# One PSUM bank for a step's transposes of p, copied by one engine in turn, and other places for two weight loads

## The chip, the cores and the metric

The kernel runs on one core of a Trainium2 chip. The metric is the device time of one execution in microseconds. Three runs of the kernel before gave 422.18, 422.83 and 426.23, a median of 422.83.

## The reference: what is computed

Three layers follow each other, all in fp32.

```
attention: B,H,S,D = 4,8,576,64; causal window of 128, bias -slope_h*(i-j)
    attn = softmax(q k^T / sqrt(D) + bias);  x = attn v          # 2304 tokens x 512
soft MoE: logits = x phi (512 x 32); dispatch = softmax over tokens, combine = softmax over slots
    slot_input = dispatch^T x;  slot_out[e] = relu(slot_input[e] w1[e]) w2[e]   # 8 experts, 512 -> 1024 -> 512
    x = combine slot_out
last layer: h = relu(x w_in) (512 x 2048);  out = (h*h) w_out
```

## The kernel before, in words

Four stages follow each other: attention, the sums that lead from the tokens to the 32 slots, the 16 + 16 weight tiles of the experts (w1, w2, 1 MB each), and the last layer, a long run of matmuls (L735).

**Attention** works on 16 pairs u (a batch and two heads). A pair has nine chunks of 64 queries. The two heads lie over each other in the 128 partitions, and a chunk looks at no more than 192 keys. Two chunks make a step, so there are 72 steps t. One step goes through all engines: TensorE makes the scores s (`emit_S`, L162); VectorE adds the bias and takes the maximum (`emit_max`, L170); ScalarE takes the exponential with its sum (`emit_exp`, L181); VectorE adds 1e-9 and inverts the sum (`emit_add` L185, `emit_norm` L189); GpSimd multiplies p by it (L194); TensorE transposes p in 128 x 128 pieces (`emit_T`, L213 to L221); and the transposes are copied from PSUM into the buffer ptb (`emit_evac`, L235 and L237). When a pair has all its steps in ptb, TensorE multiplies them with V (`emit_PV`, L247). Three steps later the result is turned back into rows (`emit_xn`: four transposes into X, L279, and one into Y, L281; VectorE copies X at L283, ScalarE copies Y at L284). After each fourth pair the logits and the dispatch sums of a batch follow (L267 to L330).

The order of every engine's work is the order in which the loop from L394 writes it down. In one turn t stand: scores of t+1, the transposes of step t-3 (LT is 3), PV where a pair is done, ScalarE's copy, the maximum of t, the sum of t-1, the exponential of t, the inverse and the multiplication of t-1, VectorE's copy, and then the side work such as `emit_xn`. Each engine takes its instructions strictly in this order.

PSUM has eight banks of 512 columns. Three of them carry the tag T, and they are handed out in turn to everything of that tag: each asks for the bank that was handed out three requests earlier, and its first matmul waits until that one has been copied out. Before, a step asks twice: `tp` gets the whole 128 x 128 pieces (one or two), `tq` the half pieces (one or two, of which 64 partitions are used). ScalarE copies `tp` with one instruction, VectorE copies `tq` with one for each half. X, Y and the second result bank of PV (`xb`) have tag T as well.

**Loads** stand in SyncE's queue. When the scores of the last chunk of pair u are made, the loop (L398 to L402) asks for q and k of pair u+2, and then for one weight tile, or two with pairs 2 and 6. V of a later pair follows after `emit_xT`. The tiles go into a ring of 19 buffers, of which the loop fills 18; the rest is asked for by `pump` when the matmuls of the experts have used a tile up. Five more w1 tiles (L82) go where the attention's buffers were.

Of the kernel before, what the change touches and what calls it, by code (L numbers as in the profile page):

```python
# [24 lines left out]
LT = 3  # L25
# [3 lines left out]
def attn_moe_relu2_kernel(ctx: ExitStack, tc: tile.TileContext, z0, q, k, v, phi, w1, w2, w_in, w_out, bias, cst, out):  # L29
# [8 lines left out]

    NBUF = {"S": 3, "T": 3, "xa": 1, "B": 1}

    def bank(tag, name):
        return psum[0].tile([128, 512], F32, tag=tag, name=name, bufs=NBUF[tag])
# [22 lines left out]
    def load_next_w():  # L65
        key = wq.pop(0)
        used[0] += 1
        if key[0] in ("w1", "w2"):
            t = ring.tile([128, 4, 512], F32, tag="w", name=f"w_{key[0]}{key[1]}")
            sp.dma_start(out=t, in_=wsrc[key[0]][key[1]].rearrange("p (a b) -> p a b", a=4))  # L70
        else:
            t = ring.tile([128, 2, 512, 2], I32, tag="w", name=f"f{key[1]}")
            for a, src in enumerate((w_in, w_out)):
                sp.dma_start(out=t[:, a].rearrange("p a b -> p (a b)"), in_=src[key[1]].bitcast(I32))
        wt[key] = t

    def load_extra(n):
        p = more.enter_context(tc.tile_pool(name=f"more{len(extra)}", bufs=n))
        for _ in range(n):
            key = extra.pop(0)  # L80
            wt[key] = p.tile([128, 4, 512], F32, tag="w", name=f"w_{key[0]}{key[1]}")
            sp.dma_start(out=wt[key], in_=wsrc[key[0]][key[1]].rearrange("p (a b) -> p a b", a=4))  # L82
# [37 lines left out]
    ptb = apool.tile([128, 4 * NBL, 128], F32, name="ptb")  # L120
# [14 lines left out]
    def load_q(u):  # L135
        z = zq[u % NQ]
        sp.dma_start(out=z[0:64, :, 0, :], in_=q[u, 0:64].rearrange("p (c t) -> p c t", t=64))
        sp.dma_start(out=z[64:128, :, 1, :], in_=q[u, 64:128].rearrange("p (c t) -> p c t", t=64))
        load_k(u)
# [7 lines left out]
    NS = NCH * NU // 2  # L147
    info = []
    for g in range(2 * NS):
        u, c = divmod(g, NCH)  # L150
# [4 lines left out]
    st_t, sb_t, xa_t, xb_t, tp_t = {}, {}, {}, {}, {}  # L155

    def emit_S(t):
        sb_t[t] = bank("S", "s")
        st_t[t] = apool.tile([128, 6], F32, tag="st", name="st", bufs=4)
        for i in range(2):  # L160
            u, c, n, e = info[2 * t + i]
            pe.matmul(out=sb_t[t][:, 256 * i:256 * i + n], lhsT=zq[u % NQ][:, c].rearrange("p a b -> p (a b)"),  # L162
                      rhs=kt_t[u][:, 64 * c + 64 - n:64 * c + 64], start=True, stop=True)

    def emit_max(t):
        for i in range(2):
            u, c, n, e = info[2 * t + i]
            p = pbuf[t % NP][:, e:e + n]
            pr = u % NPAIR
            dve.tensor_tensor_reduce(  # L170
                out=p, in0=sb_t[t][:, 256 * i:256 * i + n], in1=tbl[:, 192 * pr + 192 - n:192 * pr + 192],
                scale=-0.125, scalar=3.0e38, op0=ALU.add, op1=ALU.min, accum_out=st_t[t][:, i:i + 1],
            )
        sb_t.pop(t)

    def emit_exp(t):
        st = st_t[t]
        for i in range(2):
            u, c, n, e = info[2 * t + i]
            p = pbuf[t % NP][:, e:e + n]  # L180
            act.activation(out=p, in_=p, func=AF.Exp, bias=st[:, i:i + 1], scale=-1.0, accum_out=st[:, 2 + i:3 + i])  # L181

    def emit_add(t):
        st = st_t[t]
        dve.tensor_scalar(out=st[:, 2:4], in0=st[:, 2:4], scalar1=1e-9, scalar2=None, op0=ALU.add)  # L185

    def emit_norm(t):
        st = st_t.pop(t)
        dve.reciprocal(out=st[:, 4:6], in_=st[:, 2:4])  # L189
        for i in range(2):  # L190
            u, c, n, e = info[2 * t + i]
            p = pbuf[t % NP][:, e:e + n]
            eng = dve if t >= NS - 2 and i == 1 else pool
            eng.tensor_scalar(out=p, in0=p, scalar1=st[:, 4 + i:5 + i], scalar2=0.0, op0=ALU.mult, op1=ALU.add)  # L194
# [3 lines left out]
    def emit_T(t):  # L198
        full, half, P = [], [], pbuf[t % NP]
        for u, c, n, e in info[2 * t:2 * t + 2]:  # L200
            if c % 2:
                full.append((jblk(u, c // 2) + 1, e + n - 128))
                if n == 192:
                    half.append((64, jblk(u, c // 2 - 1) + 3, e))
            else:
                half.append((0, jblk(u, c // 2), e + n - 64))
                if n == 192:
                    full.append((jblk(u, c // 2 - 1) + 2, e))
        full.sort(key=lambda x: x[0])
        A = bank("T", "tp")[:, 0:256].rearrange("p (a b) -> p a b", a=2)  # L210
        B = bank("T", "tq")[:, 0:256].rearrange("p (a b) -> p a b", a=2)
        for i, (slot, e) in enumerate(full):
            pe.transpose(A[:, i, :], P[:, e:e + 128], ident)  # L213
        if len(half) == 2 and half[0][0] != half[1][0]:
            pe.transpose(B[:, 0, :], P[:, 128:256], ident)  # L215
            dst = [(ptb[r:r + 64, slot], B[r:r + 64, 0]) for r, slot, e in half]
        else:
            dst = []
            for i, (r, slot, e) in enumerate(half):
                assert r == 0 and e <= 256  # L220
                pe.transpose(B[:, i, :], P[:, e:e + 128], ident)  # L221
                dst.append((ptb[0:64, slot], B[0:64, i]))
        sl = [x[0] for x in full]
        st = sl[1] - sl[0] if len(sl) == 2 else 1
        if st < 0:
            raise AssertionError
        tp_t[t] = [(ptb[:, sl[0]:sl[-1] + 1:st], A[:, 0:len(sl)])], dst

    def jblk(u, j):
        return 4 * ((5 * u + j) % NBL)  # L230

    def emit_evac(t, i):
        for dst, src in tp_t[t][i]:
            if i == 0:
                act.activation(out=dst, in_=src, func=AF.Copy)  # L235
            else:
                dve.tensor_copy(out=dst, in_=src)  # L237

    def emit_PV(u):
        xa_t[u], xb_t[u] = bank("xa", "xa"), bank("T", "xb")  # L240
        for j in range(5):
            pt = ptb[:, jblk(u, j):jblk(u, j) + 4]
            for a, b in ((0, 4),) if j < 3 else ((0, 2), (2, 3)) if j == 3 else ((0, 1),):
                for h in range(2):
                    po = 64 * h
                    out = xa_t[u][po:po + 64, 128 * j + 64 * a:128 * j + 64 * b] if j < 3 or (j == 3 and a == 0) else xb_t[u][po:po + 64, 0:64]
                    pe.matmul(out=out, lhsT=v_t[u][:, j, po:po + 64], rhs=pt[:, a:b, po:po + 64],  # L247
                              start=(j == 0 or (j == 3 and a == 2)), stop=(j == 4 or (j == 3 and a == 0)), skip_group_check=True)
        xT[u] = xT_buf[u % NPAIR]
# [12 lines left out]
    def emit_logits(u):  # L262
        b, kk = divmod(u, NPAIR)
        if kk == 0:
            L_t[b] = bank("B", "L")
        for g in range(4):
# [91 lines left out]
    for u in range(NU):  # L358
# [19 lines left out]
        if u % NPAIR == NPAIR - 1:  # L378
            b = u // NPAIR
# [7 lines left out]
    def run_side(t):  # L387
        for f, a in side.get(t, ()):
            f(*a)
            if f is emit_xT and a[0] + NQ < NU:  # L390
                load_v(a[0] + NQ)

    emit_S(0)
    for t in range(NS + LT + 1):  # L394
        if t + 1 < NS:
            emit_S(t + 1)
            for u, c, n, e in info[2 * t + 2:2 * t + 4]:
                if c == NCH - 1:  # L398
                    if u + NQ < NU:
                        load_q(u + NQ)  # L400
                    for _ in range(2 if u in (2, 6) else 1):
                        load_next_w()  # L402
        if 0 <= t - LT < NS:
            emit_T(t - LT)
        for a in side0.get(t, ()):
            emit_PV(*a)
        if 0 <= t - LT < NS:
            emit_evac(t - LT, 0)
        if t < NS:
            emit_max(t)  # L410
        if 0 <= t - 1 < NS:
            emit_add(t - 1)
        if t < NS:
            emit_exp(t)
        if 0 <= t - 1 < NS:
            emit_norm(t - 1)
        if 0 <= t - LT < NS:
            emit_evac(t - LT, 1)
        run_side(t)
        if t == NS - 2:  # L420
            zt.close()
            load_extra(1)
        if t == NS + LT - 1:
            pt.close()
            load_extra(1)
# [10 lines left out]
    u, b = NU - 1, NB - 1  # L436
    p = slice(32 * b, 32 * b + 32)
# [13 lines left out]
    sl = slice(128 * kk, 128 * kk + 128)  # L451
# [448 lines left out]
```

## Time and profile before

| | |
|---|---|
| runs | 422.18, 422.83, 426.23 us |
| profiled execution | 423.25 us, its span 421.5 us |
| busy over the span | TensorE 400.4 us (95%), VectorE 293.4 (70%), ScalarE 249.7 (59%), GpSimd 94.6 (22%) |
| L213/L215/L221, transposes of p | 128 of `tp`, mean 277 ns |
| L235, ScalarE's copies of `tp` | 72, 25.3 us |
| L237, VectorE's copies of `tq` | 128, 35.4 us |
| bytes moved | 70.95 MB, mean 168 GB/s |

The profiled execution took 0.42 us more than the median of the runs. Busy time counts a matmul until its result is written, so short waits of TensorE can hide in it: a group of matmuls that could have started earlier shows as idle only what is left after the one ahead has drained.

### The profile page before, as it was taken

Reading aid. Unit: us, or ns where it says so; the run is one execution under the profiler, and the core shown is the slowest. Engines: PE = TensorE matmul, PEld = TensorE weight load, DVE = VectorE, ACT = ScalarE, POOL = GpSimd, SP = SyncE. Lnnn points to the kernel's source line nnn. Section 1 sums busy time; section 2 is a strip of 40 time slices with the busy share of each in tenths; the row PEclk is TensorE's granted clock in tenths of the full one; section 3 lists DMA queues with packets and bytes.
Section 4 is the critical chain, followed back from the end, with each engine's and each line's share of the span. In section 5 each row is a group of like instructions: output and inputs, shape, how many; then the busy total and the mean of one; then the engine's idle time right before and its main releaser. Section 6 shows DMA issues by size and latency. Waiting matters only on the chain.

```text
span 421.5 us, 7942 instructions
## 1 busy us (share of the span) xinstructions
PE 400.4 (95%) x2623; PEld 306.7 (73%) x2623; DVE 293.4 (70%) x966; ACT 249.7 (59%) x761; POOL 94.6 (22%) x193
## 2 busy tenths in 40 slices
PE   5999997999999999978999999999999999999996
PEld 4878866878867633356778788787878888888885
DVE  6887777778788426587868768677676676548445
ACT  3888876778777402057766766666666645435341
POOL 4445334244334010146112210111100000000000
PEclk9999999999999999999999999999999999999999
DMA  7979769869686799999602202000000012004004
GB/s 215 307 276 305 261 218 323 218 194 313 223 287 233 264 425 423 412 409 408 255 0 101 100 2 100 2 0 0 2 1 2 1 64 87 0 2 150 0 2 150
DMA packets 35514, 70.95 MB, mean 168 GB/s; under 512 B 19856, under 2 KB 21008, under 8 KB 31376
## 3 DMA queue, kind: packets, MB, share of 16 engines
q1 hardware_dynamic: 35328, 70.30, 47.7%
q8 instruction: 21, 0.34, 0.4%
q14 instruction: 21, 0.17, 0.1%
q10 hardware_dynamic: 144, 0.13, 0.1%
HBM read 65.70 MB, written 4.72 MB: 167 GB/s over the span
## 4 chain that ended last, share of the span: by engine, by line
PE 51%; DVE 2%; issue 1%; POOL 1%; ACT 1%; DVEq 0%; POOLq 0%
PE acc L735 45%; PE h L692 4%; PE MX L644 1%; DVE psum L753 1%; PE MY L650 1%; POOL arena_y L605 1%; DVE arena_y L621 1%; DVE arena_y L619 0%; ACT whl L637 0%; DVE Mst L653 0%; DVE arena_co L623 0%; ACT psum L745 0%; ACT siT L745 0%; DVE arena_gh L721 0%; DVEq L896 0%
## 5 line engine op out<-in xcount | busy, mean ns | idle before, releaser
L735 PE MATMUL acc<-whl,arena_gh 128*128 128x512 f32 x864 | 214.4, 396 | 2.3 <-DVE arena_gh L721 1.8
L735 PEld LDWEIGHTS acc<-whl,arena_gh 128*128 128x128 f32 x864 | 159.9, 189 | 34.8 <-issue 2.8
L721 DVE TENSOR_TENSOR arena_gh<-hT,arena_gh 128x384 fp32r<-128x384 f32 (+1 forms) x95 | 52.7, 555 | 38.5 <-ACT arena_gh L717 34.1
L194 POOL TENSOR_SCALAR p<-p,st 128x192 f32<-128x192 f32 (+1 forms) x142 | 56.1, 408 | 77.0 <-PE s L162 20.2
L704 ACT ACTIVATE acc<-h 128x384 f32<-128x384 f32 (+2 forms) x49 | 23.8, 485 | 75.0 <-PE h L692 75.0
L181 ACT ACTIVATE p<-p,st 128x192 f32<-128x192 f32 (+1 forms) x144 | 61.3, 428 | 8.0 <-DVE st L170 7.3
L162 PE MATMUL s<-kt,zq 128*128 128x192 f32 (+2 forms) x288 | 58.8, 328 | 7.4 <-DMA kt<-in_k_dram 7.0
L605 POOL TENSOR_SCALAR arena_y<-f 128x512 f32<-128x512 f32 x32 | 27.9, 875 | 120.7 <-DVE arena_cin L623 59.0
L162 PEld LDWEIGHTS s<-kt,zq 128*128 128x128 f32 x288 | 44.8, 195 | 10.1 <-DMA zq<-in_z_dram 4.6
L237 DVE COPY ptb<-tq 64x128 f32<-64x128 f32 x128 | 35.4, 281 | 22.1 <-PE tq L215 18.9
L170 DVE CUSTOM_DVE_ANT_0 p<-s,tbl 128x192 f32<-128x192 f32 (+1 forms) x144 | 41.6, 324 | 2.3 <-PE s L162 1.8
L235 ACT ACTIVATE ptb<-tp 128x256 f32<-128x256 f32 (+1 forms) x72 | 25.3, 351 | 19.4 <-PE tp L213 18.1
L247 PE MATMUL xa<-ptb,vt 128*64 128x256 f32 (+1 forms) x256 | 27.8, 359 | 0.0
L213 PE MATMUL tp<-cs,p 128*128 128x128 f32 x128 | 26.4, 277 | 1.3 <-DVE ptb L237 0.7
L181 ACT ACTIVATION_READ_ACCUMULATOR p<-p,st 128x1 f32 x144 | 27.2, 189 | 0.0
L692 PE MATMUL h<-cst_sb,Mst 128*128 128x384 f32 x96 | 25.2, 341 | 1.9 <-DVE Mst L653 1.8
L713 DVE TENSOR_TENSOR hT<-acc 128x384 f32<-128x384 f32 (+1 forms) x18 | 10.2, 566 | 23.4 <-ACT acc L704 23.4
L717 ACT ACTIVATE arena_gh<-acc 128x384 fp32r<-128x384 f32 (+2 forms) x49 | 24.9, 508 | 0.6
L717 ACT ACTIVATE arena_gh<-hT 128x384 fp32r<-128x384 f32 x48 | 24.9, 518 | 0.6
L621 DVE SCALAR_TENSOR_TENSOR arena_y<-f,arena_y 128x512 int32<-128x512 int32 x32 | 24.1, 753 | 1.1
L247 PEld LDWEIGHTS xa<-ptb,vt 128*64 128x64 f32 x256 | 17.0, 136 | 9.6 <-issue 2.4
L692 PEld LDWEIGHTS h<-cst_sb,Mst 128*128 128x128 f32 x96 | 18.1, 190 | 7.1 <-DVE Mst L653 3.3
(171 smaller groups left out, 475.3 us busy)
## 6 DMA issues: line engine op xcount, KB each, us to landing
w_w<-in_w_dram SPq DMA_DIRECT2D x32, 1024.0 KB, 8.1
f<-in_w_in_dram SPq DMA_DIRECT2D x16, 512.0 KB, 10.2
f<-in_w_out_dram SPq DMA_DIRECT2D x16, 512.0 KB, 10.2
vt<-in_v_dram SPq DMA_DIRECT2D x16, 320.0 KB, 6.2
zq<-in_q_dram SPq DMA_DIRECT2D x30, 144.0 KB, 4.3
kt<-in_k_dram SPq DMA_DIRECT2D x15, 288.0 KB, 4.4
out_dram<-psum SPq DMA_DIRECT2D x11, 256.0 KB, 2.1
out_dram<-xn_all SPq DMA_DIRECT2D x4, 256.0 KB, 2.1
```

The source lines that it names most:

```text
L162: pe.matmul(out=sb_t[t][:, 256 * i:256 * i + n], lhsT=zq[u % NQ][:, c].rearrange("p a b -> p (a b)"), rhs=kt_t[u][:, 64 * c + 64 - n:64 * ...
L170: dve.tensor_tensor_reduce(out=p, in0=sb_t[t][:, 256 * i:256 * i + n], in1=tbl[:, 192 * pr + 192 - n:192 * pr + 192], scale=-0.125, scalar ...
L181: act.activation(out=p, in_=p, func=AF.Exp, bias=st[:, i:i + 1], scale=-1.0, accum_out=st[:, 2 + i:3 + i])
L194: eng.tensor_scalar(out=p, in0=p, scalar1=st[:, 4 + i:5 + i], scalar2=0.0, op0=ALU.mult, op1=ALU.add)
L237: dve.tensor_copy(out=dst, in_=src)
L247: pe.matmul(out=out, lhsT=v_t[u][:, j, po:po + 64], rhs=pt[:, a:b, po:po + 64], start=(j == 0 or (j == 3 and a == 2)), stop=(j == 4 or (j ...
L605: pool.tensor_scalar(out=y[:, a].bitcast(F32), in0=t[:, a, :, 1].bitcast(F32), scalar1=2.0 ** -112, scalar2=0.0, op0=ALU.mult, op1=ALU.add)
L621: dve.scalar_tensor_tensor(out=y[:, h], in0=t[:, h, :, 1], scalar=-0x80000000, in1=y[:, h], op0=ALU.bitwise_and, op1=ALU.bitwise_or)
L692: pe.matmul(out=hb[hf][:, 0:HB], lhsT=Mst[:, 128 * f:128 * f + 128], rhs=cst_sb[:, c0:c0 + HB], start=True, stop=True)
L717: act.activation(out=lo_t[i][1][hf][:, 0, cl], in_=rbuf[hf][:, cl], func=AF.Square)
L721: eng.tensor_tensor(out=gh[hf][:, 1, cl], in0=g[hf][:, cl], in1=gh[hf][:, 0, cl].bitcast(F32), op=ALU.subtract)
L735: pe.matmul(out=acc_t[s], lhsT=gh[:, x, c0:c0 + 128], rhs=w[:, f % 2, y, :], start=(f in firsts and a == 0), stop=(f in lasts and a == 2))
```

## The change

Both kinds of pieces of a step now lie in one bank, whole ones in columns 0 to 255 and half ones in columns 256 to 511, so a step asks once for a bank of tag T. All copies of an even step are made by ScalarE, where its copy stood, and all copies of an odd step by VectorE, where its copies stood. The second weight tile of a turn is asked for with pairs 7, 11 and 13 in place of 2 and 6, so 19 tiles are in the ring when the attention ends.

```diff
-        A = bank("T", "tp")[:, 0:256].rearrange("p (a b) -> p a b", a=2)
-        B = bank("T", "tq")[:, 0:256].rearrange("p (a b) -> p a b", a=2)
+        AB = bank("T", "tp").rearrange("p (x a b) -> p x a b", x=2, a=2)
+        A, B = AB[:, 0], AB[:, 1]
...
-        tp_t[t] = [(ptb[:, sl[0]:sl[-1] + 1:st], A[:, 0:len(sl)])], dst
+        tp_t[t] = [(ptb[:, sl[0]:sl[-1] + 1:st], A[:, 0:len(sl)])] + dst
...
-    def emit_evac(t, i):
-        for dst, src in tp_t[t][i]:
-            if i == 0:
+    def emit_evac(t):
+        for dst, src in tp_t.pop(t):
+            if t % 2 == 0:
                 act.activation(out=dst, in_=src, func=AF.Copy)
             else:
                 dve.tensor_copy(out=dst, in_=src)
...
-                    for _ in range(2 if u in (2, 6) else 1):
+                    for _ in range(2 if u in (7, 11, 13) else 1):
                         load_next_w()
...
-        if 0 <= t - LT < NS:
-            emit_evac(t - LT, 0)
+        if 0 <= t - LT < NS and (t - LT) % 2 == 0:
+            emit_evac(t - LT)
...
-        if 0 <= t - LT < NS:
-            emit_evac(t - LT, 1)
+        if 0 <= t - LT < NS and (t - LT) % 2:
+            emit_evac(t - LT)
```

VectorE in the turns 32 and 33 of the loop, from the sum of step 31 to the copy of X of pair 5 (p_96 is p of step 33; `tq` and `tp` are the transposes of step 29, then of step 30). Before:

```order
L185 TENSOR_SCALAR st<-st 128x2
L189 RECIPROCAL st<-st 128x2
L237 COPY ptb<-tq 64x128 x2
L170 ISA p_96,st<-s,tbl 128x192
L170 ISA st 128x1
L170 ISA p_96,st<-s,tbl 128x192
L170 ISA st 128x1
L185 TENSOR_SCALAR st<-st 128x2
L189 RECIPROCAL st<-st 128x2
L237 COPY ptb<-tq 64x128 x2
L283 COPY xn_all<-X 128x4x128
```

And now:

```order
L185 TENSOR_SCALAR st<-st 128x2
L189 RECIPROCAL st<-st 128x2
L237 COPY ptb<-tp 128x2x128
L237 COPY ptb<-tp 64x128 x2
L170 ISA p_96,st<-s,tbl 128x192
L170 ISA st 128x1
L170 ISA p_96,st<-s,tbl 128x192
L170 ISA st 128x1
L185 TENSOR_SCALAR st<-st 128x2
L189 RECIPROCAL st<-st 128x2
L283 COPY xn_all<-X 128x4x128
```

The odd step 29 now has three copies here where it had two, and the even step 30 has none.

ScalarE in the turns 31 to 33 at the same place, from pair 5's result to the exponentials of step 32 (p_94 is step 31, p_95 step 32; the copies are of steps 28, 29 and 30). Before:

```order
L256 ACTIVATE xT_100<-xb 128x64
L235 ACTIVATE ptb<-tp 128x2x128
L181 ACTIVATE p_94,st<-p_94,st 128x192
L181 ACTIVATE p_94,st<-p_94,st 128x64
L235 ACTIVATE ptb<-tp 128x2x128
L181 ACTIVATE p_95,st<-p_95,st 128x128
L181 ACTIVATE p_95,st<-p_95,st 128x192
L235 ACTIVATE ptb<-tp 128x2x128
```

And now:

```order
L256 ACTIVATE xT_100<-xb 128x64
L235 ACTIVATE ptb<-tp 128x2x128
L235 ACTIVATE ptb<-tp 64x128 x2
L181 ACTIVATE p_94,st<-p_94,st 128x192
L181 ACTIVATE p_94,st<-p_94,st 128x64
L181 ACTIVATE p_95,st<-p_95,st 128x128
L181 ACTIVATE p_95,st<-p_95,st 128x192
L235 ACTIVATE ptb<-tp 128x2x128
L235 ACTIVATE ptb<-tp 64x128 x2
```

Two half copies now stand ahead of the exponentials of the odd step 31, and no copy stands ahead of those of step 32.

## Rows read from the trace of the kernel before

**Rows 1.** Windows by stage: busy us (instructions) of each engine, granted clock, DMA share, GB/s.

```profile
3.00:140.00 137.00, 128.95 (x1137) 103.69 (x1138) 105.48 (x598) 101.53 (x422) 56.17 (x143) 1.00 0.83 259
148.20:178.80 30.60, 30.57 (x273) 10.06 (x274) 13.86 (x46) 3.68 (x9) 3.51 (x4) 1.00 1.01 420
197.00:421.00 224.00, 219.41 (x1065) 177.83 (x1064) 152.77 (x277) 129.14 (x291) 21.73 (x25) 1.00 0.14 54
```

**Rows 2.** Timeline, GpSimd: the first work on the last layer's weights.

```profile
176.59 0.68 POOL L605 TENSOR_SCALAR arena_y<-f 128x512 f32<-128x512 f32 x1 [19.36 <-DMA f<-in_w_in_dram]
```

**Rows 3.** Waits of TensorE, 3 to 140 us: total, times, longest.

```profile
PE s L162 <- DMA kt<-in_k_dram: 7.0, 4, 3.4
PE X L279 <- DVE ptb L237: 1.8, 8, 0.3
PE tp L213 <- DVE ptb L237: 0.7, 3, 0.2
PE tq L215 <- DVE ptb L237: 0.3, 2, 0.2
```

**Rows 4.** Timeline, SyncE's queue and TensorE around pair 6's second weight tile: start, us.

```profile
58.28 1.24 SPq L70 DMA_DIRECT2D w_w<-in_w_dram  x2
...
63.26 0.54 SPq L137 DMA_DIRECT2D zq<-in_q_dram  x1
...
70.99 0.54 SPq L137 DMA_DIRECT2D zq<-in_q_dram  x1
...
73.05 0.41 PE L162 MATMUL s<-kt,zq 128*128 128x64 f32 x2 [2.10 <-DMA kt<-in_k_dram]
...
81.63 0.55 SPq L137 DMA_DIRECT2D zq<-in_q_dram  x1
```

**Rows 5.** Timeline, TensorE: X and Y of pair 5, transposes of steps 31, 32.

```profile
61.84 0.63 PE L279 MATMUL X<-cs,xT 128*128 128x128 f32 x4 [0.19 <-DVE ptb L237]
62.30 0.27 PE L281 MATMUL Y<-cs,xT 128*128 128x128 f32 x1
...
63.28 0.30 PE L213 MATMUL tp<-cs,p 128*128 128x128 f32 x1
...
64.10 0.38 PE L213 MATMUL tp<-cs,p 128*128 128x128 f32 x2
```

**Rows 6.** Timeline, VectorE, same steps.

```profile
59.72 0.59 DVE L237 COPY ptb<-tq 64x128 f32<-64x128 f32 x2 [1.39 <-PE tq L215]
...
61.12 0.57 DVE L237 COPY ptb<-tq 64x128 f32<-64x128 f32 x2
...
62.48 0.17 DVE L189 RECIPROCAL st<-st 128x2 f32<-128x2 f32 x1
62.56 0.57 DVE L237 COPY ptb<-tq 64x128 f32<-64x128 f32 x2
```

**Rows 7.** Timeline, ScalarE and GpSimd, same steps.

```profile
59.61 0.38 ACT L235 ACTIVATE ptb<-tp 128x256 f32<-128x256 f32 x1 [0.47 <-PE tp L213]
59.89 0.45 ACT L181 ACTIVATE p<-p,st 128x192 f32<-128x192 f32 x1
...
60.57 0.19 ACT L181 ACTIVATION_READ_ACCUMULATOR p<-p,st 128x1 f32 x1
...
62.81 0.77 POOL L194 TENSOR_SCALAR p<-p,st 128x128 f32<-128x128 f32 x2 [0.70 <-ACT p L181]
```

**Rows 8.** Groups by shape: count, busy us, mean ns.

```profile
L283 DVE COPY xn_all<-X 128x512 f32<-128x512 f32 x15 | 10.3, 685 | 0.8 <-PE X L279 0.6
L284 ACT ACTIVATE xnr<-Y 128x128 f32<-128x128 f32 x15 | 3.9, 261 | 5.0 <-PE Y L281 5.0
L312 DVE COPY dn<-X 128x128 f32<-128x128 f32 x3 | 0.8, 273 | 0.0
```

**Rows 9.** Timeline, VectorE and TensorE: the same place of pair 2, whose step there is odd.

```profile
37.43 0.59 DVE L237 COPY ptb<-tq 64x128 f32<-64x128 f32 x2
...
38.17 0.30 PE L213 MATMUL tp<-cs,p 128*128 128x128 f32 x1 [0.22 <-DVE ptb L237]
```

## The prediction, made before the changed kernel ran

> **What bounds the kernel now.** I began with the windows by stage. In the attention, 3 to 140 us, TensorE is busy 128.95 of 137 us while no other engine passes 105.48, and its clock is full [rows 1]: TensorE's own instructions set the pace and the others have room, on average. From 148 to 179 us the 32 weight tiles run one behind the other (30.57 busy of 30.60), and from 197 us to the end it is again TensorE without holes [rows 1]. Between those two lies a start-up chain of the last layer whose first input is a transfer, at 176.59 us [rows 2]. So nothing behind the attention gets shorter by this change, and whatever the attention gains or loses goes through to the end. The transfers behind it keep up: the first weights of the last layer arrive 2.2 us before the weight matmuls end (178.80), and the change only brings one tile, about 2.5 us of transfer at the 420 GB/s of that window, forward. I price that tile at nothing at the end; its cover is those 2.2 us, and the change makes them longer.
>
> What TensorE waits for inside the attention is the second thing read [rows 3]. Of K it waits 7.0 us in four places. Most of this is the start and stays; one place is 2.10 us at 73.05 us [rows 4]. For banks it waits 1.8 us at eight X, 0.7 us at three `tp` and 0.3 us at two `tq`. That is only the visible part: before X at 61.84 TensorE was idle for 0.19 us, but the copy that released it ended at 61.12 + 0.57 = 61.69, so a release takes 0.15 us, and the transposes ahead were draining in that time.
>
> Third, the queues at one such place [rows 5 to 7]. X of pair 5 waits for VectorE's copies of step 29. The next `tp` at 63.28 waits for those of step 30, which end at 62.56 + 0.57 = 63.13, plus the same 0.15. So the banks that hurt belong to the step directly ahead, not to an old one.
>
> **Part 1, weight tiles.** Pair 6 asks for two tiles at 58.28; q and K for pair 9 are asked for from 63.26 on and TensorE gets K at 73.05, 2.10 us late and 0.15 of drain with it [rows 4]: 2.25 us that go, because pair 6 now asks for one. Pair 7 asks for two instead. The next q and K (for pair 10) are asked for at 70.99 and needed at 81.63, which contains the 2.1: 8.5 us, where the late case had 73.05 - 2.25 - 63.26 = 7.5 and took 9.8 [rows 4]. With the same transfers K would still be 2.25 - 1.0 = 1.25 us late; but the second tile of pair 2 made no wait of that size at all [rows 3], where 3.4 is the start and 2.1 of the rest is pair 6's, with the same loads around it. Between 0 and 1.25 I take the nearer row, pair 2, and put 0.25 us of new waiting for pairs 7 and 11 together (bounds 0 and 2 x 2.25), nothing for pair 13, behind which no q and K follow. Net -2.0 us.
>
> **Part 2, the copies' prices.** VectorE never copies 256 columns in the trace. Nearest rows: 128 columns 273 ns, 512 columns 685 ns [rows 8]; on the line between them 0.41 us (bounds 0.27 and 0.69). ScalarE never copies a half; its 128-column copy takes 261 ns [rows 8], and as its next instruction starts 0.1 us before the end (59.89 against 59.61 + 0.38 [rows 7]) a half occupies it 0.16 us. So ScalarE has 0.32 us more in an even step and 0.28 less in an odd one, VectorE about 0.4 more in an odd one and 0.57 less in an even one. Per two steps the sums hardly move; the order does.
>
> **Part 3, where X follows an even step (pair 5).** Carried through with these prices. ScalarE starts step 28's copies when the last transpose is done, 59.72 (there VectorE began on it [rows 6]) instead of 59.61, and is through with them 0.28 + 0.32 later: the exponentials of step 31 begin at 60.32, not 59.89, and end at 60.57 + 0.19 + 0.43 = 61.19 [rows 7]. VectorE, rid of step 28's copies, stands early before the sum of step 31 and waits for them. Then sum and inverse (0.28), and step 29's copies run from 61.5 to 61.5 + 0.41 + 0.57 = 62.48, against 61.69 before. X no longer needs this bank; now X takes step 28's, and Y takes step 29's. Y goes at 62.63, not 62.30 [rows 5]. Y and the scores behind it take 0.76 us (before, `tp` could have gone at 63.06 and waited 0.22 for its bank), so the next `tp` comes at 63.39 against 63.28: its own wait is gone, and Y's has eaten it. VectorE's inverse of step 32 stands behind step 29's copies and the maximum of 33, and slips from 62.48 to about 63.26; GpSimd follows 0.33 later and needs 0.77 for both halves [rows 6, 7], so the second piece of step 32, wanted 0.11 behind the first at 64.10 + 0.11, is there at 64.36 plus 0.12 for the release. Together the place costs 0.27 us **more** than before: 0.11 at the bank and 0.16 at p.
>
> **Part 4, where it follows an odd step (pair 2).** VectorE's copies for the step start at 37.43 and release `tp` at 38.17 [rows 9]. Now two turns ahead it has 0.4 more, one turn ahead 0.57 less, and the sum waits for exponentials that ScalarE's whole copy has pushed back: the start stays at about 37.4, and with 1.0 us in place of 0.59 plus 0.15 for the release `tp` comes at 38.5. Cost 0.33 us.
>
> Eight places have a wait at X [rows 3]: pairs 0, 1, 5, 9, 13 (even) and 2, 6, 10 (odd) by the parity of the step (9u+8)//2+4. 5 x 0.27 + 3 x 0.33 = +2.3 us. The other pairs have dispatch sums of a batch before or behind X, long matmuls in which VectorE and ScalarE catch up.
>
> **Part 5, what does vanish.** Where a step's `tq` waited for ScalarE's copy of the step before, or for an old copy of VectorE, the next bank is now free: 0.3 us visible in two places plus up to 0.15 of drain each, and more that hides in drain. I take -1.0 us (bounds -0.3 and -2).
>
> **Sum.** -2.0 + 2.3 - 1.0 = -0.7 on the profiled 423.25 us, and this execution lies 0.42 over the median of 422.83: 422.1 us as a median. The sign rests on parts 3 and 4, in which terms of 0.3 us repeat eight times; an error of 0.25 in each is 2 us.
>
> By the Trainium skill, "Perfetto Trace Analysis", section "Optimization Strategy", the same gap that repeats on the engine that should be saturated can mean that there is not enough PSUM for the next tile. The trace has that gap eight times [rows 3]; by that rule one bank less per step removes it, which is the first rival. What speaks against is the release time: 0.15 us behind the copies of the step just ahead.
>
> **Rivals.** (a) **The bank waits go.** If ScalarE's halves delay nothing because exponentials run in holes, then at all eight places the wait at X (1.8 us + 8 x 0.15 = 3.0) and the one behind it (63.28 against about 62.9 without, some 0.3 x 7 = 2.1) disappear. -5.1 - 2.0 - 1.0 = -8.1: 414.7 as a median; half of it 418.8. For it: averages of 74 to 77% for both engines [rows 1]. Against: the carried queues, in which the place of the wait moves by one request. Chance 0.28.
>
> (b) **Slower: p comes late.** Exponentials pushed back (0.43) and long copies of odd steps (0.41) both stand ahead of the inverse, which GpSimd and the transposes of p await. Before, p of step 32 was ready at 62.81 + 0.77 = 63.58, 0.5 ahead of its transposes at 64.10 [rows 5, 7]. If the two delays add up, 0.84 - 0.5 = 0.34, and the bank's 0.33 comes on top, in all 14 pairs with X: +9.4 - 2.0 - 1.0 = +6.4, 429.2. It decides where the delay is over 0.5 us. Chance 0.13.
>
> (c) **K late twice.** If pairs 7 and 11 each cost what pair 6 did, +4.5 - 2.25 + 1.3 = +3.5: 426.4. For it speaks that q and K stand behind two tiles in one queue; by the Trainium skill, "DMA: Bandwidth & Descriptors", section "Queues, rings and completion order", each engine consumes a row's ring in order, so the K has to wait for both, and the late K here agrees (9.8 us from request to use [rows 4]). Against: 8.5 us of room, not 7.5. Chance 0.07.
>
> That leaves 0.52 for the forecast, within 419.5 to 424.5.
>
> **The numbers.** Predicted 422.0 us. Range 416.5 to 426.5: it cuts off the far part of (a), about 0.1, and most of (b), the same. 1% (4.2 us) is about what a measurement of this kernel can tell from no change. Faster by more, below 418.6: (a) but for its weak end, 0.25. Slower by more, over 427.1: (b), 0.12. Within: 0.63.
>
> **What would show it.** In the changed profile: TensorE's K wait at pair 9 gone and none above 0.5 us at pairs 10 and 14; Y, not X, waiting for VectorE's L237 after even steps, for about 0.3 us, and `tp` behind Y after odd ones; ScalarE busy about 4 us more and VectorE about 4 less in the attention; the weight matmuls beginning 0 to 2 us ahead of 148.2; the stages behind unchanged in length. Wrong: no bank waits left and the attention 5 us shorter, or waits of the transposes for GpSimd's p in most pairs.

## The result and the profile after

The changed kernel takes **425.75 us** (median of 22 runs, 424.88 to 427.7) against 422.76 of the kernel before in the same runs (22 runs, 421.3 to 426.23): a ratio of 1.0068, 95% interval 1.0052 to 1.0085. That is 3.0 us more; forecast was 422.0, no change. The profiled span is 423.9 us, before 421.5.

The windows by stage, of the changed kernel, with the columns of [rows 1] (the second and third are moved with their stages, which begin later):

```profile
3.00:140.00 137.00, 124.01 (x1114) 102.20 (x1116) 102.38 (x567) 106.82 (x449) 56.54 (x143) 1.00 0.82 265
150.00:180.60 30.60, 30.54 (x273) 10.04 (x273) 14.30 (x47) 3.56 (x9) 3.71 (x4) 1.00 0.99 399
199.40:423.40 224.00, 219.40 (x1065) 177.86 (x1065) 152.65 (x277) 129.21 (x291) 21.76 (x25) 1.00 0.14 51
```

The two later stages are what they were: 30.54 of 30.60 us and 219.40 of 224. In the attention TensorE is busy 5 us less in the same 137 us, with fewer instructions done by then; VectorE has 3.1 us less and ScalarE 5.3 us more than in [rows 1] (forecast: about 4 each way). From the first scores to the first weight matmul the attention and the sums behind it take 146.2 us, before 144.8. Beside these 1.4 us the start is 0.4 later (K at 3.86 us, before 3.44), and the stretch behind the weight matmuls is 0.6 longer, for a reason that the last section tells. Together 2.4, the difference of the spans.

What TensorE waits for, 3 to 142 us, of the changed kernel (total, times, longest), to be held against [rows 3]:

```profile
PE s L162 <- DMA kt<-in_k_dram: 3.9, 1, 3.9
PE Y L281 <- DVE ptb L237: 3.7, 5, 0.8
PE R L318 <- DVE dn L312: 3.5, 3, 1.2
PE tp L213 <- ACT xnr L284: 3.1, 3, 1.0
PE s L162 <- POOL p L194: 0.7, 1, 0.7
PE tp L213 <- POOL p L194: 0.5, 1, 0.5
```

K is late no more but at the start (the 0.7 us for `p` lie in the start too, at 9.66 us). X waits nowhere; **Y** waits at the five places behind an even step, and **tp** at the three behind an odd one, as forecast, though for more. And there is a wait that stands in no row of before: **R**, three times, for `dn`.

**The place behind an even step (pair 5)**, timeline of the changed kernel, ScalarE, VectorE, TensorE in turn:

```profile
60.93 0.82 ACT L235 ACTIVATE ptb<-tp 128x256 f32<-128x256 f32 x3 [0.58 <-PE tp L215]
61.77 0.45 ACT L181 ACTIVATE p<-p,st 128x192 f32<-128x192 f32 x1
...
62.69 0.17 DVE L185 TENSOR_SCALAR st<-st 128x2 f32<-128x2 f32 x1 [1.40 <-ACT p L181]
...
62.97 0.90 DVE L237 COPY ptb<-tp 128x256 f32<-128x256 f32 x3
...
64.02 0.30 PE L281 MATMUL Y<-cs,xT 128*128 128x128 f32 x1 [0.73 <-DVE ptb L237]
```

This is the chain of the prediction's third part. ScalarE copies a whole step (0.82 us) ahead of the exponentials, VectorE's sum waits 1.40 us for them, its three copies stand behind the sum, and Y gets the bank 0.15 us after their end (62.97 + 0.90 = 63.87).

**The place behind an odd step (pair 2)**, same engines:

```profile
35.97 0.95 ACT L235 ACTIVATE ptb<-tp 128x256 f32<-128x256 f32 x3 [0.96 <-PE tp L215]
...
36.82 0.44 ACT L181 ACTIVATE p<-p,st 128x192 f32<-128x192 f32 x1
...
38.58 0.26 ACT L284 ACTIVATE xnr<-Y 128x128 f32<-128x128 f32 x1
...
38.12 1.02 DVE L237 COPY ptb<-tp 128x256 f32<-128x256 f32 x3
...
38.98 0.30 PE L213 MATMUL tp<-cs,p 128*128 128x128 f32 x1 [1.03 <-ACT xnr L284]
```

Here the trace corrects the description ahead of the prediction. The next `tp` does not take the bank of the step directly ahead, whose copies end only at 38.12 + 1.02 = 39.14, but Y's: it starts 0.14 us after ScalarE's copy of Y ends (38.84). So the banks of tag T are not always handed out in strict turn. Y's copy is late for the same kind of reason: four exponentials stand ahead of it on ScalarE, from 36.82 to 38.67, and ahead of them the whole-step copy.

**The new wait at R**, changed kernel:

```profile
51.36 0.95 ACT L235 ACTIVATE ptb<-tp 128x256 f32<-128x256 f32 x3
...
53.06 0.17 DVE L185 TENSOR_SCALAR st<-st 128x2 f32<-128x2 f32 x1 [1.27 <-ACT p L181]
...
53.34 1.00 DVE L237 COPY ptb<-tp 128x256 f32<-128x256 f32 x3
54.27 0.27 DVE L312 COPY dn<-X 128x128 f32<-128x128 f32 x1
...
54.60 1.06 PE L318 MATMUL R<-xn_all,dn 128*32 128x512 f32 x8 [1.10 <-DVE dn L312]
```

and the same place before:

```profile
52.39 0.59 DVE L237 COPY ptb<-tq 64x128 f32<-64x128 f32 x2
52.90 0.27 DVE L312 COPY dn<-X 128x128 f32<-128x128 f32 x1
...
53.42 1.06 PE L318 MATMUL R<-xn_all,dn 128*32 128x512 f32 x8
```

`dn`, the small copy that the dispatch sums R need, stands in VectorE's queue behind the odd step's three copies, and these behind a sum that waited 1.27 us for exponentials, which stood behind ScalarE's whole-step copy. Before, two short copies stood ahead of `dn`, and R began without a wait for it.

### The profile page after: what moved, and what is told of

Its sections match the earlier page's. It is cut to its first block, busy times and chain, and to the rows that moved or that the text cites. A ratio compares the mean times of both kernels' runs of the same rounds, so it can differ in the third digit from the quotient of the medians.

```text
span 423.9 us, 7965 instructions
## 1 busy us (share of the span) xinstructions
PE 398.5 (94%) x2623; PEld 307.2 (72%) x2623; DVE 291.2 (69%) x938; ACT 255.5 (60%) x789; POOL 94.9 (22%) x193
## 4 chain that ended last, share of the span: by engine, by line
PE 52%; DVE 2%; ACT 1%; issue 0%; DVEq 0%
PE acc L735 46%; PE h L692 4%; PE MX L644 1%; DVE psum L753 1%; PE MY L650 1%; DVE arena_y L621 1%; DVE arena_y L619 0%; ACT whl L637 0%; DVE arena_gh L721 0%; DVE Mst L653 0%; DVE arena_co L623 0%; ACT psum L745 0%; ACT siT L745 0%; DVEq L896 0%; ACT Mst L652 0%
## 5 line engine op out<-in xcount | busy, mean ns | idle before, releaser
L237 DVE COPY ptb<-tp 64x128 f32<-64x128 f32 (+2 forms) x100 | 29.5, 318 | 8.1 <-PE tp L215 7.5
L235 ACT ACTIVATE ptb<-tp 64x128 f32<-64x128 f32 (+2 forms) x100 | 27.0, 298 | 12.9 <-PE tp L215 8.6
L213 PE MATMUL tp<-cs,p 128*128 128x128 f32 x128 | 26.5, 277 | 3.7 <-ACT xnr L284 3.1
```

## The experiments

My theory after the traces: two things happen to the queues. A whole-step copy on ScalarE delays the exponentials, and with them VectorE's sum; a whole-step copy on VectorE then delays what stands behind it. The banks of Y and `tp` and the `dn` of R come late by this, and the saved K wait is swallowed. The rivals: the weight tiles cost something; one bank for both kinds of pieces is what costs; or no single wait matters and the attention is simply full.

**The tiles alone.** The kernel before, with the second tile at the new pairs:

```diff
-                    for _ in range(2 if u in (2, 6) else 1):
+                    for _ in range(2 if u in (7, 11, 13) else 1):
```

> The kernel before with only the weight tiles moved (second tile with pairs 7, 11, 13). Theory (the copies in the queues cost, the tiles gain): the K wait of 2.1 us for pair 9 goes, none over 0.5 us comes at pairs 10 and 14: 2.0 us faster than before, 420.8 us. Rival (the tiles' new places are what costs): 2 to 4 us slower than before, with K waits in pairs 10 and 14.

421.93 us (421.02 to 423.12), ratio to the kernel before 0.9982 [0.9966, 0.9999]. The sign was right, the size too large: by the interval the gain is at most 1.4 us, where 2.0 had been expected. In the trace the 2.1 us wait at pair 9 is gone (from the scores of step 40 to those of step 41 it takes 1.93 us less), 0.4 are lost again later (K, at step 63), and 0.6 went to the slower clock of the last section. The first step of the prediction holds for the kernel before, at about 1.5 us.

**The copies alone.** The change with the tiles left at pairs 2 and 6, the edit above turned back.

> The changed kernel with the weight tiles as before (pairs 2 and 6). Theory: the waits of the changed kernel for banks and for dn (Y 3.7, tp 3.1, R 3.5 us) stand, and the K wait of about 2 us is back: 427.7 us, 5 us over before. Rival (the tiles cost): like before, 422.8 us, or less.

425.6 us, ratio 1.0068 [1.0045, 1.0091]: missed. It is as slow as the whole change, so on top of the copies the tiles bring nothing: from the scores of step 10 to those of step 71 both traces take 115.2 us (the kernel before 112.9). The reason stands at the first scores of pair 9, of the copies alone:

```profile
72.86 0.41 PE L162 MATMUL s<-kt,zq 128*128 128x64 f32 x2 [0.66 <-DMA kt<-in_k_dram]
73.38 0.30 PE L213 MATMUL tp<-cs,p 128*128 128x128 f32 x1
```

and of the whole change:

```profile
73.39 0.30 PE L213 MATMUL tp<-cs,p 128*128 128x128 f32 x1 [1.02 <-ACT xnr L284]
```

With the copies alone K is still late there, by 0.66 us in place of 2.10: it lands at 72.73 us, in the kernel before at 72.92, but the new waits make the pairs longer, and TensorE comes to it 1.2 us later. What is left of the lateness costs nothing, because the `tp` behind it is held up by its bank until the same moment in the whole change, where K is in time: 73.38 and 73.39. The terms of my sum were not independent.

**The copies of `dn` moved.** The changed kernel, `emit_d2` (which writes `dn`) directly behind the maximum, ahead of the sum and of VectorE's copies of the same turn:

```diff
-            add(8, emit_d2, b)
+            early.setdefault(t0 + 8, []).append(b)
...
             emit_max(t)
+        for x in early.get(t, ()):
+            emit_d2(x)
```

> The changed kernel with the two transposes of dT and VectorE's two copies into dn written right behind the maximum of their turn, ahead of the sum and of the long copy. Theory: dn is ready while VectorE waits for the exponentials anyway; R's wait of 3.5 us in three places falls under 0.5: 3 us faster than the changed kernel, 422.7 us. Rival (R's bank, not dn, is what it waits for, or the wait passes on to the next transposes): within 0.7 us of the changed kernel.

422.04 us, ratio 0.9979 [0.9958, 1.0]. Two small copies in each of three batches (`dn`, 0.27 and 0.17 us), moved with their transposes ahead of one long copy, give back 3.7 us. The waits of this kernel:

```profile
PE Y L281 <- DVE ptb L237: 3.7, 5, 0.8
PE s L162 <- DMA kt<-in_k_dram: 3.5, 1, 3.5
PE tp L213 <- ACT xnr L284: 3.1, 3, 1.0
...
```

R is off the list, and the two bank waits stand unchanged to the tenth. From the scores of step 10 to those of step 71 this trace takes 111.7 us, the changed kernel's 115.2: 3.5 us less, as much as R had waited. So the wait at R went through one for one.

**A fourth bank for T.** The changed kernel with four banks of tag T; the bank comes from tag B, whose users get others:

```diff
-    NBUF = {"S": 3, "T": 3, "xa": 1, "B": 1}
+    NBUF = {"S": 3, "T": 4, "xa": 1}
...
-            L_t[b] = bank("B", "L")
+            L_t[b] = bank("S" if b == NB - 1 else "T", "L")
...
-    W = bank("B", "W")
+    W = bank("S", "W")
```

> The changed kernel with four banks of tag T: the logits' bank, which had a tag of its own, asks for a bank of T (the last batch's for one of S). Theory (Y and the transposes behind it wait because only three banks rotate, and the one they get belongs to a step that VectorE is just copying): these waits, 3.7 and 3.1 us visible, go; up to 2 us of them come back as waits for p; R's 3.5 us for dn stay, since that is data and not a bank. 5 us faster than the changed kernel, 420.7 us. Rival (the copies and exponentials are behind anyway, p is the limit): the waits turn into waits for GpSimd's p, less than 2 us faster.

422.16 us, ratio 0.9961 [0.9933, 0.9989], 3.6 us less than the changed kernel, where 5 had been expected. In its waits the bank waits of Y and `tp` are gone, R's stands:

```profile
PE R L318 <- DVE dn L313: 3.8, 3, 1.3
PE s L162 <- DMA kt<-in_k_dram: 3.5, 1, 3.5
PE tp L213 <- POOL p L194: 0.9, 1, 0.9
PE G L466 <- DVE bm L449: 0.8, 1, 0.8
...
PE tp L213 <- DVE ptb L237: 0.2, 1, 0.2
```

From the scores of step 10 to those of step 71 the 5 us came as expected (110.3 us, the changed kernel 115.2). Behind them 1.0 us is lost again up to the first weight matmul, and a wait stands there that the list of the changed kernel does not have, of G for `bm`.

By the Trainium skill, "Perfetto Trace Analysis", section "Optimization Strategy", the same gap that repeats on the engine that should be saturated can mean that there is not enough PSUM for the next tile. This run agrees: one bank more, and 6.8 us of visible waits at eight places go. Asking once per step in place of twice, with three banks, had not done it.

**Both mends.** The two edits above together.

> Four banks of tag T and the dn copies ahead of the long copy, both on the changed kernel. Theory: the two gains are of different places and add up, 5 + 3.7: 417.0 us, faster than both kernels. Rival: K or p become the limit and half of it is lost, 421 us.

418.19 us (417.92 to 418.59), ratio 0.9871 [0.9832, 0.9909]. The gains add (3.6 + 3.7 = 7.3; measured 7.6). Beside the start, no wait of TensorE inside the attention is longer than 0.9 us. And with the tiles back at pairs 2 and 6:

> The same with the second weight tiles at pairs 2 and 6 as in the kernel before. Theory (K is late only where the pairs run fast; in the changed kernel the other waits had covered it, so that moving the tiles brought nothing there): with those waits gone K of pair 9 is late again by 2 us and more: 419.3 us, 2.3 us slower than with pairs 7, 11, 13. Rival (where the tiles stand never matters beside the copies): no difference, 417.0 us.

419.33 us, ratio 0.991 [0.9875, 0.9945]. The waits for K, here and then with the new pairs:

```profile
PE s L162 <- DMA kt<-in_k_dram: 5.0, 3, 3.5
```

```profile
PE s L162 <- DMA kt<-in_k_dram: 3.6, 2, 3.4
```

Where the pairs run fast, the place of the tiles matters again, by 1.1 us, half of what was expected: TensorE waits for K 1.12 us at 38.8 and 0.41 at 71.45. The intervals of the two runs overlap, so it is the traces that show it (108.2 against 106.7 us from the scores of step 10 to those of step 71). This and the copies alone are two sides of one thing: what a transfer costs depends on how long the pair is that covers it, and on what else TensorE would wait for at that place.

**Parity turned.** The changed kernel with ScalarE on the odd steps and VectorE on the even ones:

```diff
-            if t % 2 == 0:
+            if t % 2:
                 act.activation(out=dst, in_=src, func=AF.Copy)
```

and the two conditions in the loop likewise.

> The changed kernel with the parity turned: ScalarE copies odd steps, VectorE even ones. Theory (long copies stand in VectorE's queue ahead of what TensorE waits for): R no longer waits for dn, whose copies of VectorE no longer stand behind a long copy (3.5 us less in three places); of the eight places with X five instead of three wait at tp (1.0 us visible) and three instead of five at Y (0.7): plus 0.6. Sum 2.7 us faster than the changed kernel, 423.0 us. Rival (one bank for a step, or ScalarE's whole copies, cost in any parity): 425.7 us as the changed kernel, R still waiting.

423.35 us, ratio 1.0019 [1.0001, 1.0037]: as expected. The step ahead of `dn` is odd in all three batches, so its copies are now ScalarE's; R's wait is gone, and the bank waits have changed places:

```profile
PE tp L213 <- ACT xnr L284: 4.9, 5, 1.0
PE s L162 <- DMA kt<-in_k_dram: 3.5, 1, 3.5
PE Y L281 <- DVE ptb L237: 2.3, 3, 0.8
```

The bank waits go with the parity of the step, and their sum hardly moves (7.2, changed kernel 6.8).

**Parity turned, with a fourth bank.** If the theory is right, this needs no second mend.

> The change with a fourth bank of tag T and the parity turned (ScalarE odd, VectorE even steps). Theory: both kinds of wait go without moving the dn copies, since the turn of R then has no long VectorE copy: R under 1 us, Y and tp under 1 us in sum, 425.7 - 3.6 - 2.4 = 419.7, possibly as low as 418.5. The rival (the turned parity only moved the waits to the banks and gains nothing of its own): 422, as with the fourth bank alone.

417.38 us (417.04 to 419.04), ratio 0.9849 [0.9813, 0.9885]. It beats both kernels and lies 2.3 us under what was expected; its interval overlaps with that of both mends. R's wait is gone without the copies of `dn` being moved. The bank waits, expected under 1 us, still make 1.8:

```profile
PE tp L213 <- ACT xnr L284: 1.3, 4, 0.6
...
PE tp L213 <- DVE ptb L237: 0.5, 3, 0.2
```

**One half of the copy change at a time.** The change does two things: one bank for a step, and one engine for a step. Engine by parity, but two banks:

```diff
-        AB = bank("T", "tp").rearrange("p (x a b) -> p x a b", x=2, a=2)
-        A, B = AB[:, 0], AB[:, 1]
+        A = bank("T", "tp")[:, 0:256].rearrange("p (a b) -> p a b", a=2)
+        B = bank("T", "tq")[:, 0:256].rearrange("p (a b) -> p a b", a=2)
```

> The change with its copies by parity, but the pieces of a step lie in two banks again, as before the change. My theory (the long copies on one engine are what costs; one bank instead of two saves little): R's three waits for the dn copies stay at about 3.5 us, the bank waits at Y, X and tp are as large or larger in sum than after the change, 425.5 to 427.5. The rival (putting both kinds of pieces into one bank is what costs, because the bank comes free only with the last of three copies): the waits at X shrink towards those of the kernel before, and the time falls to about 423.5.

430.38 us (429.67 to 432.16), ratio 1.0157 [1.0119, 1.0195]. Slower than the theory gave it, and R's wait did not stay, which I had expected. The waits:

```profile
PE tq L215 <- DVE ptb L237: 3.8, 9, 0.6
PE s L162 <- DMA kt<-in_k_dram: 3.5, 1, 3.5
PE Y L281 <- DVE ptb L237: 2.8, 3, 0.9
PE tq L221 <- POOL p L194: 1.4, 4, 0.3
PE tp L213 <- DVE ptb L237: 1.3, 3, 0.4
PE X L279 <- ACT ptb L235: 0.7, 4, 0.2
```

With two requests per step the long copies hold up `tq` in the middle of the steps as well. R is not awaited for `dn` because TensorE comes to it later: in the first batch the transposes directly ahead of R wait 0.44 and 0.21 us for VectorE's copies, and R starts at 56.78 us, when `dn` is written (56.67). So the wait has not gone, it stands one group of instructions earlier.

One bank, but the engines by kind of piece as before (and the new pairs for the tiles): the edit above the other way round, in the kernel with the tiles alone.

> One bank for the pieces of a step and the tiles with pairs 7, 11 and 13, but the copies by kind of piece as in the kernel before (ScalarE the whole ones, VectorE the halves, in every step). It is the fourth cell of a square: two banks and kind 421.9 (the tiles alone), two banks and parity 430.4, one bank and parity 425.75. Theory: one bank is worth about 4.6 us and parity costs about 8.5 us, each by itself, so 421.9 - 4.6 = 417.3; in the trace the waits at X are gone (X takes the bank of a step that was copied one turn earlier), R waits under 0.6 us for dn. The rival: one bank pays only where one engine copies the whole step, because otherwise the bank waits for the later of two engines; then the waits at X stay and the time is about 422.

426.33 us (425.27 to 427.32), ratio 1.0075 [1.0044, 1.0106]. It missed by 9 us; the rival's 422 missed as well. All four cells have the new pairs for the tiles:

| | two banks a step | one bank a step |
|---|---|---|
| engine by kind of piece | 421.93 (0.9982) | 426.33 (1.0075) |
| engine by parity | 430.38 (1.0157) | 425.75 (1.0068) |

Neither half pays by itself. One bank costs 4.4 us where the engines copy by kind, and takes 4.6 off what two banks cost where they copy by parity. With one bank these runs show no difference between the two rules for the engines (the intervals are 1.0044 to 1.0106 and 1.0052 to 1.0085). For the upper right cell the waits of VectorE and ScalarE show what has changed:

```profile
DVE ptb L237 <- ACT ptb L235: 24.6, 20, 1.8
...
ACT ptb L235 <- PE tp L215: 12.4, 16, 1.3
```

Where each kind has its bank (the tiles alone), these rows read

```profile
ACT ptb L235 <- PE tp L213: 17.7, 30, 1.4
...
DVE ptb L237 <- PE tq L215: 19.0, 18, 1.4
```

With two banks each engine is released by the transposes that it copies, ScalarE already by the whole pieces (L213), and they copy at once. With one bank ScalarE is released only by the last transpose of the bank (L215), and VectorE by the end of ScalarE's copy: one after the other. In none of the 72 steps does VectorE begin before ScalarE has ended (0.03 us behind it in many), where with the tiles alone it begins ahead of that end in 24, by 0.27 us in most of these. What enforces this order the runs do not show. That they are two engines then helps no more, and R waits 2.9 us for `dn` here too.

**The kernel before with the mends.** Four banks and the new pairs, copies by kind into two banks:

> The kernel before (two banks a step, both engines copying each step) with four banks of tag T and the weight tiles at 7, 11, 13. Theory: the eight waits at X and most of those at the transposes behind it go, 4 us of the 421.9 us that the moved tiles alone gave: 418 us, and no long copies: no more than 1 us from the changed kernel with both mends. Rival (one bank a step is what saves banks, two banks a step need more than four): under 2 us of gain, 420 us.

420.56 us, ratio 0.9926 [0.9899, 0.9954]: 2.6 over what was expected, and near the rival's 420. Its X waits for no bank, but `tq` still waits 2.2 us for VectorE's copies and 1.3 for p. And with the copies of `dn` moved ahead as above:

> The kernel before with the fourth bank, tiles with pairs 7, 11 and 13, and the dn copies ahead of the sum; copies by kind of piece as before. It asks whether copying by parity brings anything once its waits are mended. Theory (its order keeps p and the banks later for tq, whose waits of 3.5 us the kernel with fourth bank and tiles alone still showed): R's wait of 0.5 us goes, the rest stays, 420.3. The rival (parity brings nothing, the mends do all): 418.2, as with the change and both mends.

419.54 us, ratio 0.9889 [0.9849, 0.9928]. This lies between the two expectations, and its interval overlaps with those of the change with both mends (0.9832 to 0.9909) and of the turned parity with four banks (0.9813 to 0.9885). What the change brings by itself, once its waits are mended, is some 1 to 2 us of these 420 by the medians, anything from nothing to 5 by the intervals: these runs do not settle it.

## Why the prediction was wrong

- **What bounds the kernel**: right for the stages. What the attention lost went through to the end; the weight tiles and the last layer kept their lengths. Inside the attention the averages of the engines misled: TensorE is busy 5 us less in the same time, because it waits.
- **Part 1, tiles, -2.0 us**: right in sign in the kernel before, about 1.5 us. In the changed kernel the wait at pair 9 is gone too and the term comes out (-1.9), but **the tiles are not its cause there**: the copies alone take it away as well. I priced the tiles against a pair of the old length, and the other parts changed this length and put a second wait at the same place.
- **Part 2, prices of the copies**: VectorE's 256 columns take 411 ns, mean of 28 (estimate 0.41). ScalarE's halves I put at 0.16 us each, from a copy with an exponential behind it. Behind another copy they mostly start 0.27 to 0.29 apart, and the exponentials begin 0.84 us behind the first copy of the step (60.93 to 61.77) in place of 0.28 + 0.32 = 0.60: this was 0.24 short. The sums over the attention, 5.3 more and 3.1 less, were near.
- **Parts 3 and 4, the eight X places, +2.3 us; measured +3.2**: the mechanism held behind even steps, place by place (Y in place of X, 0.15 us behind VectorE's copies). Three of the five cost 0.5 us each where 0.27 had been forecast, and ScalarE's 0.24 would account for that. Behind odd steps `tp` was late as said, 0.35 us a place (forecast 0.33), but by ScalarE's copy of Y and not by the copies of the step ahead. There the number was luck.
- **The step that failed: "The other pairs have dispatch sums ... in which VectorE and ScalarE catch up".** This put R's places at nothing. There the two delays of the first three parts meet ahead of a small copy that TensorE needs at once: it waits 1.1 to 1.2 us in three batches, 3.5 in all. Held against the kernel before, whose `tq` is held up a little at the same places, they are 2.2 us longer. Moving that copy gives 3.7 us back and brings the time to 422.04, where I had forecast 422.0 for the whole change. I had carried the queues through at two places and taken the rest from an average.
- **Part 5, small bank waits, -1.0 us**: right in size. The `tq` waits are gone with `tq`, and the places of X in pairs 3, 7 and 11, at which the list of waits shows nothing, are 0.38 us shorter each.

From the starts of the scores in the two traces, the changed kernel's against those of the kernel before, in us up to the first weight matmul (K and the odd place of pair 6 fall together and are told apart by the trace of the tiles alone):

| | forecast | traces |
|---|---|---|
| K of pair 9 (part 1) | -2.0 | -1.9 |
| X, five even places | +1.35 | +2.1 |
| X, three odd places | +1.0 | +1.0 |
| places of X in pairs 3, 7, 11 (part 5) | -1.0 | -1.1 |
| R, three places | 0 | +2.2 |
| the first ten steps | 0 | -0.55 |
| behind the scores of step 71 | 0 | -0.4 |
| sum | -0.7 | +1.4 |

Without R the sum would have come out near the forecast, in part by chance: what the X places cost beyond their price is balanced by the last two terms. Of these the first is no doing of the change that I can show (the copies alone and the whole change, the same program up to there, differ by 0.4 us in it), and the second stays open.

- **Rivals**: (a), the bank waits go, is refuted with three banks; with four they do go, for 3.6 us. (b), p late in all pairs, is refuted: the transposes wait once for GpSimd, 0.5 us. (c), K late twice, is refuted, though its 426.4 is the number nearest to the one measured. The case that came, a small copy behind a long one, was none of them, though it is made of the same two delays as (b).

The range, 416.5 to 426.5, holds the 425.75, and so does "within 1%", but the difference is clear and on the side to which I gave the smaller chance.

## What to carry to other kernels

Merging copies onto one engine leaves the sums of work nearly as they were and lengthens what stands ahead of everything else in that engine's queue: go through every kind of turn and look at the smallest instruction behind the merged one that the bounding engine needs, and move it ahead. A repeated wait for a PSUM bank went with one bank more, not with one request less; and two engines that copy out of one bank may take turns, so look at who releases the second. Terms of a sum that are waits of one loop are not independent: a late transfer disappears when something else makes the loop longer or holds up the same place, and comes back when that is mended.

## What the runs showed of the hardware

Behind the weight matmuls TensorE has gaps. The longest ahead of the last layer is 1.81 us in the changed kernel (up to 188.65) and 1.79 in the kernel before (up to 186.81); at its end in the first, and 1.1 us behind it in the second, the granted clock falls to the lower of its two levels, 1.2 GHz, for a stretch. The length of that stretch goes with no kernel. Windows of the changed kernel, the stretch and the one ahead of it:

```profile
188.40:195.20 6.80, 6.15 (x22) 4.34 (x23) 4.71 (x9) 2.50 (x7) 3.49 (x5) 0.50 1.02 407
187.00:188.40 1.40, 0.00 (x0) 0.00 (x0) 1.31 (x3) 0.70 (x3) 1.40 (x2) 0.98 1.04 416
```

and of the kernel before, the stretch and the one behind it:

```profile
187.90:191.40 3.50, 3.10 (x8) 2.54 (x9) 2.16 (x5) 1.90 (x5) 2.20 (x3) 0.51 1.03 407
191.40:194.70 3.30, 2.16 (x17) 1.48 (x15) 3.23 (x5) 2.33 (x5) 1.62 (x2) 1.00 1.02 410
```

Of the 14 profiles, seven have 3.4 us at half clock and seven 6.8, over the same instructions. From the end of the weight matmuls to the end of the span it takes 242.4 to 242.9 us in the first seven and 243.0 to 243.3 in the others, on average some 0.6 us more. The kernel before and the copies alone are of the first kind, the change, the tiles alone and both best kernels of the second, with no relation to what was edited that I can see. Differences of single profiles below 1 us are therefore taken from the attention alone here, not from the span.
